# New engine orders, banks and P buffers for a linear-plus-softmax attention mixed with a token MLP; two stores issued by ScalarE

## The chip, the cores and the metric

The kernel runs on one core of one Trainium2 chip. The metric is device time in microseconds of one execution; lower is better. Five engines work side by side and meet through semaphores: TensorE (PE, with its weight loads shown apart as PEld), VectorE (DVE), ScalarE (ACT), GpSimd (POOL) and SyncE (SP), which here only issues DMAs.

## The reference

Two branches read the same 2048 x 448 input `x` and are mixed by a gate for each row. Cut to what matters (16 heads of 28, four segments of 512 rows):

```python
g = sigmoid((x * gate_w).sum(-1, keepdims=True))
# branch A: attention in segments, with a memory of the earlier ones
q, k, v = x @ wq, x @ wk, x @ wv                     # heads, 4 segments of 512
for s in range(4):
    p = softmax(qs @ ks.T * Dh**-0.5 + causal_mask)
    a_dot = p @ vs
    a_mem = (phi(qs) @ M) / (phi(qs) @ z + 1e-6)     # phi(t) = t+1 if t>0 else exp(t)
    o = sigmoid(beta) * a_mem + (1 - sigmoid(beta)) * a_dot
    M, z = M + phi(ks).T @ vs, z + phi(ks).sum()
a = concat(o) @ wo
# branch B: layernorm over 448, then an MLP over the 2048 tokens
u = gelu_tanh(einsum('bsd,sf->bdf', layernorm(x), w1) + b1)   # 448 x 1792
b = (einsum('bdf,fs->bds', u, w2) + b2).T
out = g * a + (1 - g) * b
```

## The kernel before

Everything of one execution is recorded as some 1300 named operations; `ORDER` (from line 288 on) then says, for each engine, in which order it issues them. The order is written out by hand or by a program, not worked out when the kernel is built: `plan` reads the words, `finalize` puts semaphore waits where an operation needs one of another engine. An engine issues strictly in its list's order, so an operation that waits holds up all that stand behind it on its engine. A word like `u3-11*4` means four consecutive operations, `@5` the PSUM bank (or, for `exp`, the P buffer) that the operation takes, `#1` the second operation of that name.

The names that the change and the steps below touch:

- `sc{p}_{f}` on PE (L955): fill `f` (0 to 4) of a pair `p` (0 to 7) of score tiles, four matmuls side by side on 28-row parts of the array, 512 columns, into the four PSUM banks 0 to 3. All 40 fills take these same four banks. `exp{p}_{f}` on ACT (L964) reads all four banks in one instruction of 2048 columns and writes P to one of six P buffers (three more become free in the place of transposed input). `mask{p}_{f}_{j}` on POOL (L967) zeroes the upper triangle of a diagonal block.
- `pv{u}` on PE (L991) multiplies P by V, `mem{u}` reads the memory, `mst{s}` (L830) updates it. `ta{u}`, `tm{u}` (L1007, L1005) transpose the two results on DVE; `eps`, `rec`, `oa`, `om` (L1016 to L1020) and `o{u}` on POOL (L1022) combine them, and `ot{u}` (L1028) transposes the result back. `wo{T}` on PE is the output projection of a 128-row tile `T`; `ag{T}` (L1048 on ACT, L1052 on DVE) takes it out of PSUM with the gate.
- `lo..`, `hi..`, `pr..` on PE: parts of the Q, K and V projections (`lok3_0`, `prq3_1`, `lot10` ...), with `cpk`, `cpq`, `cpv` (L718, L778, L800 and their DVE forms) as evictions. `gt` is the tanh of the gate. `ek`, `eq` (L761, L785) on ACT are the exps of phi for K and Q; `mk`, `phk`, `mq`, `phq` on DVE finish phi.
- `u{ft}-{st}` on PE (L264): the 16 matmuls of 448 columns of each of 14 column tiles of the first MLP product; `ev{ft}` (L1068 on ACT, L1070 on DVE) adds the bias and takes the tile out of PSUM. Three operations on ACT apply Gelu to several tiles at once (L1072): `gl0` to tiles 0 to 4, `gl5` to 5 to 9, `gl10` to 10 to 13. In the trace a load of a function table (`ACT_TABLE_LOAD`) stands ahead of each Gelu and ahead of the next Exp behind it.
- `y{T}-{ft}` on PE: the 14 matmuls of each of 16 output tiles of the second product. `fin{T}` (L1086) on DVE adds the two branches; `out{T}` (L1090) stores the tile by DMA, issued by SP. Tile 15 is made in two parts, columns 0 to 319 and 320 to 447 (`y15-..`, `fin15`, `out15`, and the same names with `#1`).
- `ldw1_{k}_{part}`, `ldw2_{k}_{part}` on SP (L557): quarter loads of the MLP weights into a ring of three slots. `gk..`, `gq..` (L742) gather the last four rows of each head through DRAM, and wait for the copies of K or Q.

A run of whole-array operations that holds a `pv` or `mst` (which use the array in four column tiles) is issued in column tiles too: each matmul then becomes four instructions of 32 columns of weights side by side. `WIDE` (line 286) names two runs which are issued so although they hold none.

Of the kernel before, what the change touches and what calls it, by code (L numbers as in the profile page):

```python
# [5 lines left out]
ACT = mybir.ActivationFunctionType  # L6
# [273 lines left out]
def pool_cost(n):  # L280
# [5 lines left out]
WIDE = ("y1-4", "y0-10",)  # L286
# [3 lines left out]
warm@4 trx0_0@16 warm2 lok0_0@53 trx0_1@72 trx0_1#1 hik0_0 lok0_0h@76 lok0_2@02 hik0_0h hik0_2 lox0_3@41 gtr@6 loq0_1@35 hix0_3  # L290
lot2@67 hiq0_1 hit2 lok1_2@24 loq1_2@01 lok1_0@35 hiq1_2 hik1_0 hik1_2 loq1_0@76 lot0@50 hiq1_0 hit0 lot4@21 lot6@43
hit4 lok2_2@76 btr@0 hit6 prk2_2 prx2_3 u1-0@5 sc0_0@0123 u0-0@4 u1-1 u0-1*2 u1-2*3 u0-3 u1-5 u0-4 u1-6 sc0_1@0123
lok2_0@67 u0-5 prk2_0 prk2_1 u0-6*2 sc0_2@0123 u0-8 u1-7 u0-9 u2-0@6 u1-8 u0-10 u2-1 u1-9*2 u0-11 u2-2 u1-11 u2-3
sc0_3@0123 u2-4 u1-12*2 u0-12 u1-14 u5-0@7 u0-13*2 u5-1 u1-15 u2-5 sc0_4@0123 u0-15 u5-2*2 pv0@5 u2-6*2 u3-0@4 u2-8*2
sc1_0@0123 u2-10 u5-4*2 u4-0@5 u3-1 u2-11 u3-2 u2-12 u4-1 u3-3 u2-13*2 u4-2 sc1_1@0123 u3-4 u5-6*2 u3-5 u5-8 u2-15
u3-6 u4-3 u3-7 u4-4*2 sc1_2@0123 u3-8 u4-6*2 pv1@6 u5-9 u3-9*2 u4-8 u5-10 sc1_3@0123 u3-11 u5-11 u3-12*2 u4-9 u5-12
u3-14*2 u4-10 u6-0@6 u5-13 sc1_4@0123 u7-0@4 u5-14 u6-1 u7-1 u6-2 u4-11 u7-2 u4-12*2 u5-15 u7-3 sc2_0@0123 u6-3 u4-14
u7-4 u4-15 u7-5*2 u6-4*2 u7-7 mst0@7 pv3@0 u6-6 pv2@3 u6-7*3 u7-8 u6-10 loq2_0@57 sc2_1@0123 u7-9 u6-11*3 u7-10 u6-14
prq2_0 u6-15 prq2_1 u7-11*4 sc2_2@0123 loq2_2@75 u8-0@6*2 u7-15 prq2_2 u8-2*5 sc2_3@0123 u8-7*6 prq2_2h u8-13*3
sc2_4@0123 wo1@4 pv4@5 u9-0@6*2 mem4@7 u9-2 sc3_0@0123 u9-3*3 wo0#1@5 u9-6*5 sc3_1@0123 lot8@57 u9-11*5 prt9 prt8  # L300
wo2@0 u10-0@6 u11-0@4 wo3@2 u11-1*2 u10-1 pv5@3 u11-3 u10-2*2 mem5@7 u11-4*3 sc3_2@0123 lot10@57 u10-4 prt11 u10-5
u11-7 prt10 u10-6*2 sc3_3@0123 u12-0@7 u11-8*2 u10-8 u11-10 u10-9 mem6@5 u11-11 u10-10*2 u11-12 sc3_4@0123 u11-13
u12-1 u11-14 u10-12 u12-2 u10-13 u12-3 u13-0@5 u10-14 u11-15 u10-15 sc4_0@0123 u13-1*2 pv6@4 u12-4 u13-3 mem7@6 u12-5
u13-4 u12-6 sc4_1@0123 mst1@4 u13-5*3 u12-7 u13-8*2 u12-8*2 sc4_2@0123 u12-10 pv7@6 u12-11 u13-10*2 u12-12 u13-12
u12-13*2 sc4_3@0123 lok3_0@46 prk3_0 u13-13 u12-15 prk3_1 u13-14 sc4_4@0123 lok3_2@47 u13-15 prk3_2 prx3_3 loq3_0@65
sc5_0@0123 prq3_1 prq3_0 wo7@4 wo5@7 wo4@1 wo6@3 pv8@4 mem8@5 mem9@6 y0-0@7*4 sc5_1@0123 y0-4*2 y2-0@5*3 y0-6 y2-3
y1-0@6*2 y2-4*2 pv9@4 y1-2*2 sc5_2@0123 y1-4 y2-6 y4-0@4*3 y2-7 y0-7*2 y4-3 y0-9 y4-4 y2-8*3 y1-5 sc5_3@0123 y0-10*2
y2-11*2 y1-6*2 y2-13 y1-8*3 y4-5 sc5_4@0123 y0-12*2 y4-6 y1-11*2 y3-0@5 y1-13 y3-1*3 y4-7 sc6_0@0123 y4-8 mem10@6
y5-0@7 y3-4 y4-9 y5-1*2 y4-10 pv10@6 sc6_1@0123 y5-3 y3-5 y5-4 y3-6*3 mem11@6 y3-9 y4-11 y5-5 y4-12 sc6_2@0123 y5-6
y3-10*2 y5-7*4 y4-13 pv11@6 sc6_3@0123 y3-12 y5-11 y7-0@4 y5-12 y7-1 y3-13 y5-13 y6-0@6 y7-2*3 loq3_2@21 lot14@03  # L310
prq3_2 prq3_2h prt14 y7-5*2 prt15 y7-7 y6-1 mst2@5 y7-8 y6-2 sc6_4@0123 lot12@75 y6-3*3 prt13 prt12 y7-9 y6-6*3
sc7_0@0123 y6-9 y7-10 y6-10 y8-0@7 y6-11 y8-1*2 y6-12 y7-11 y6-13 pv12@5 y8-3 y7-12 sc7_1@0123 y7-13 y8-4 wo8@6 pv13@5
mem12@4 y8-5 sc7_2@0123 y8-6 y10-0@6*3 mem13@4 y8-7*3 y10-3 y11-0@5 y8-10 sc7_3@0123 y10-4*2 y11-1 y10-6*2 y11-2 y8-11
wo9@4 y11-3*2 y8-12 sc7_4@0123 y8-13 y11-5 wo11@4 y11-6 pv14@7 y10-8 y12-0@1 y9-0@2 y11-7*2 y13-0@3 y9-1*4 y13-1 y10-9
y9-5 y10-10 mem14@7 y13-2 mem15@0 y11-9 y12-1 wo10@4 y9-6 y13-3 y12-2 y9-7 y10-11 y12-3 y13-4 y9-8 y11-10 pv15@7
y12-4*2 y9-9 y12-6*2 y9-10*2 y12-8 y13-5 y14-0@7 y11-11*2 y14-1 y15-0@0 y9-12 y11-13 y13-6 y9-13 y10-12*2 y14-2*2
y15-1 y13-7 y15-2 y14-4 y12-9 y13-8*2 y15-3 y14-5 y13-10 y12-10 y14-6 y15-4 y14-7 y12-11 y14-8 y13-11*3 y14-9 wo14@5
y14-10 wo12@6 y15-5 y14-11 wo13@5 y12-12 y14-12*2 wo15@6 y15-6*2 y12-13 y15-8*6 y15-0#1@4 y15-1#1 y15-2#1 y15-3#1
y15-4#1 y15-5#1 y15-6#1 y15-7#1 y15-8#1 y15-9#1 y15-10#1 y15-11#1 y15-12#1 y15-13#1
""",  # L320
    "ACT": """
ldx1 ldwkb padx0 xTcp0_01 padx1 xTcp0_11 padq1 cpk0_0 cpk0_2#1 ek0_1 cpk0_0#1 cpq0_2 cpq0_0 gt2 gt3 ln0 cpk1_1 ek0_0
cpk1_3 cpk1_2 cpk1_0 cpq1_2#1 cpq1_3 cpv1 cpq1_1 cpq1_0 gt1 cpv0 gt0 cpv4 gt5 gt4 cpv6 gt6 gt7 cpk2_2 ln7 exp0_0@6
eq1_2 exp0_1@1 cpk2_0 eq1_0 tb exp0_2@5 ln12 exp0_3@7 ek0_2 exp0_4@3 eq1_1 exp1_0@2 eq1_3 mg exp1_1@4 ek0_3 exp1_2@1
exp1_3@6 ek1_0 exp1_4@0 ek1_1 exp2_0@5 gl0 exp2_1@3 ev6 exp2_2@6 ek1_2 exp2_3@4 eq2_0 exp2_4@2 eq2_2 exp3_0@1 ek1_3
exp3_1@5 gl5 gt8 gt9 ek2_0 exp3_2@6 gt11 gt10 exp3_3@3 eq2_1 exp3_4@2 ev11 exp4_0@4 ek2_1 exp4_1@8 exp4_2@7 exp4_3@3
exp4_4@1 cpk3_3 exp5_0@2 gl10 ag4 eq3_0 exp5_1@5 eq2_3 ek2_3 exp5_2@6 exp5_3@3 ek2_2 exp5_4@0 exp6_0@8 eq3_1 exp6_1@2
exp6_2@7 exp6_3@6 eq3_2 cpv15 gt15 gt14 exp6_4@3 gt13 gt12 exp7_0@0 exp7_1@4 eq3_3 exp7_2@3 exp7_3@5 exp7_4@2 ag10
ag15
""",  # L330
    "DVE": """
wo0 padx2 padk2 padk0 xTcp0_00 padk1 bns1 xTcp0_10 bns3 padq0 padq2 cpk0_1 padq3 bns0 bna1 cpk0_1#1 cpk0_2 gw bna0
bns2 bna2 bna3 vpe0 cpk0_3 cpq0_3 cpq0_1 nmr0 cpv2 ln1 ln3 cpv3 ln2 bns5 bns7 cpq1_2 bna5 bns4 bns8 bns10 bns6 bna4
bna8 bns13 bns15 bns11 bna15 bna6 bna7 bns14 vpe4 bns9 bna11 cpv5 b1c b2c nmr4 cpv7 bna9 bna10 vpe8 mk0_0 bns12 cpk2_3
ln4 bna13 ln5 nmr8 ln6 cpq2_3 ln8 phk0_0 bna12 mk0_1 ln9 bna14 ln10 phk0_1 vpe12 cpk2_1 osl ln11 mq1_2 nmr12 ln15 ln13
ln14 maskg0 ev1 ev0 ta0 mk0_2 oc phk0_2 gm mo mq1_1 ev2 rec0 ob0 oa0 mk0_3 gcol0 mq1_3 ta1 phk0_3 ot0 ev3 mk1_0 rec1
phk1_0 oa1 ev5 ot1 omg0 ev4 mq1_0 mstc0 b2g0 gcol1 msta0 ta3 ta2 rec3 phq1_3 phq1_2 phq1_0 rec2 oa2 cpq2_0 cpq2_1 oa3
mk1_1 ev7 cpq2_2 phk1_1 ot2 ot3 cpq2_2#1 mk1_2 ev8 phk1_2 ta4 mq2_0 ag1 tm4 phq1_1 ag0 eps4 rec4 ev9 oa4 cpv9 mq2_2
ag2 cpv8 ag3 omg1 mk1_3 b2g1 ta5 tm5 phq2_0 phk1_3 om4 eps5 cpv11 cpv10 rec5 om5 oa5 tm6 mq2_1 ot4 ev10 ot5 ta6 eps6
mk2_0 rec6 phk2_0 mk2_1 om6 phq2_1 tm7 oa6 eps7 phk2_1 msta1 ta7 rec7 om7 oa7 cpk3_0 ev12 cpk3_1 ev13 cpk3_2 ot7 gcol2  # L340
ot6 cpq3_3 cpq3_1 ag7 cpq3_0 mstc1 ag5 ag6 tm8 ta8 tm9 eps8 rec8 phq2_2 eps9 omg2 ta9 mq3_0 rec9 oa8 om9 mk2_3 phk2_3
mq2_3 oa9 om8 phq2_3 fin2 fin0 fin1 tm10 ot8 eps10 ta10 rec10 mk2_2 tm11 oa10 phk2_2 phq3_0 fin4 mq3_1 ta11 om10 fin3
fin5 ot10 cpq3_2 eps11 cpq3_2#1 cpv14 b2g2 ot9 msta2 phq3_1 rec11 oa11 om11 cpv13 cpv12 mq3_2 phq3_2 mstc2 fin6 ot11
ta12 fin7 ag8 tm12 eps12 ta13 tm13 rec12 eps13 mq3_3 oa12 rec13 ag9 gcol3 om12 fin8 om13 ta14 oa13 phq3_3 ag11 tm14
tm15 eps14 ot13 eps15 ot12 rec14 oa14 ta15 rec15 om15 oa15 om14 omg3 b2g3 ot14 fin9 fin10 fin11 ot15 ag14 ag12 ag13
fin14 fin13 fin12 fin15 fin15#1
""",
    "POOL": """
hm0 id0 v0 hm1 hm2 z3_1 id1 mhalf szb z3_0 szg v1 rstd0 rstd4 hs0 hs27 rstd8 rstd12 mask0_2_2 mask0_1_1 mask0_0_0
mask0_2_2#1 mask0_1_3 mask0_4_1 mask0_4_3 mask0_3_0 mask1_2_2 mask1_0_0 mask1_2_2#1 mask1_3_0 mask1_1_1 mask1_4_1  # L350
mask1_1_3 mask1_4_3 mask2_1_1 mask2_2_2 mask2_0_0 mask2_1_3 mask2_2_2#1 mask3_0_0 mask2_4_1 mask2_4_3 mask3_1_1
mask2_3_0 o4 mask3_1_3 o5 mask3_2_2 mask3_2_2#1 mask3_4_1 mask3_4_3 mask3_3_0 o6 o7 mask4_1_1 mask4_3_0 mask4_4_1
mask4_2_2 mask4_0_0 mask4_1_3 mask4_4_3 mask4_2_2#1 mask5_2_2 mask5_1_1 o8 mask5_0_0 mask5_1_3 mask5_4_1 mask5_2_2#1
mask5_3_0 mask5_4_3 o9 mask6_1_1 mask6_2_2 mask6_1_3 o10 mask6_0_0 o11 mask6_3_0 mask6_2_2#1 mask6_4_1 mask6_4_3
mask7_1_1 mask7_2_2 mask7_1_3 mask7_0_0 mask7_2_2#1 o12 mask7_4_1 mask7_4_3 o13 mask7_3_0 o14 o15
""",
    "SP": """
# [14 lines left out]
def build_kernel(nc, X, WQ, WK, WV, WO, BETA, W1, B1, W2, B2, GW, OUT):  # L372
    NSL, NP = 3, 6
    sch = Sched(nc, {}, {})
    op = sch.op

    x2 = X.rearrange("b s d -> (b s) d")
    out2 = OUT.rearrange("b s d -> (b s) d")
# [45 lines left out]
    outst = sb([128, 4, D])  # L424
# [4 lines left out]
    b1c = sb([128, NFT], F32)  # L429
    b2c = sb([128, NT], F32)  # L430
# [644 lines left out]
    def mm2(T, c0=0, c1=D):  # L1075
# [3 lines left out]
        p = T % 4  # L1079
# [136 lines left out]
```

## Time and profile before

| | us |
|---|---|
| median of 3 runs | 173.01 |
| the runs | 172.37, 173.01, 173.29 |
| the profiled execution's own time | 173.29 |
| its span, first to last instruction | 171.6 |

Of the 40 slices of the span PE is at 80% or more in every one but the last, where it drops to three tenths, and the mean granted TensorE clock is 1.000:

```profile
PE   8899999999999999999999999999999999999993
PEld 3465444444446444453454355544455544566662
DVE  2599999844879998799789999786898996999783
ACT  2434899999899999997997899978846676410010
POOL 8011041455164043432643580079260826542300
DMA  5989795695744944780307547014865265024213
```

Each digit is the busy share of a fortieth of the span, 4.3 us, in tenths. The score fills and their exps lie between the seventh and the thirty-fifth slice, the projections ahead of them, the last MLP tiles behind. The groups of instructions that cost most on ACT and DVE:

```profile
L964 ACT ACTIVATE t<-t 128x2048 bf16<-128x2048 f32 x40 | 75.0, 1876 | 12.3 <-PE t L955 10.3
L1007 DVE STREAM_TRANSPOSE t<-t 128x512 f32<-128x512 f32 x16 | 11.2, 704 | 1.8 <-PE t L991 1.7
L1028 DVE STREAM_TRANSPOSE t<-t 128x512 bf16<-128x512 bf16 x16 | 11.0, 698 | 0.1
```

After the bar stand the busy time in us, the mean of one instruction in ns, then the idle time ahead of the group and what ended it.

### The profile page before, as it was taken

What the parts mean: (1) busy time and instruction counts of PE and PEld (TensorE: products, weight loads), DVE (VectorE), ACT (ScalarE), POOL (GpSimd) and SP (SyncE); (2) the same over time, 40 slices, a digit from 0 to 9 for tenths busy, and PEclk for the clock granted to TensorE, in tenths of its full rate; (3) what the DMA queues carried; (4) which work ended last, traced back from release to release, by engine and by line L of the source; (5) the groups of instructions that cost most, each with busy time, mean ns of one, the idle gap of its engine ahead of it and who ended that gap; (6) DMA issues with size and microseconds to landing.
All of it is one profiled execution on the core that took longest, in us unless ns stands there. A gap on an engine that the chain in (4) does not pass through costs nothing.

```text
span 171.6 us, 5965 instructions
## 1 busy us (share of the span) xinstructions
PE 167.1 (97%) x2571; PEld 85.2 (50%) x2571; DVE 145.1 (85%) x313; ACT 121.7 (71%) x126; POOL 65.6 (38%) x98
## 2 busy tenths in 40 slices
PE   8899999999999999999999999999999999999993
PEld 3465444444446444453454355544455544566662
DVE  2599999844879998799789999786898996999783
ACT  2434899999899999997997899978846676410010
POOL 8011041455164043432643580079260826542300
DMA  5989795695744944780307547014865265024213
GB/s 167 286 158 317 192 285 170 165 262 136 208 120 122 178 94 108 171 237 2 97 0 143 153 140 188 4 31 136 248 181 156 85 188 175 4 61 149 67 57 107
DMA packets 50474, 24.66 MB, mean 144 GB/s; under 512 B 14976, under 2 KB 50208, under 8 KB 50448
## 3 DMA queue, kind: packets, MB, share of 16 engines
q1 hardware_dynamic: 50160, 24.05, 53.9%
q8 instruction: 20, 0.33, 0.8%
q10 hardware_dynamic: 288, 0.23, 0.6%
q14 instruction: 6, 0.05, 0.1%
HBM read 18.76 MB, written 2.36 MB: 123 GB/s over the span
## 4 chain that ended last, share of the span: by engine, by line
PE 91%; DVE 4%; DMA 3%; SPq 0%; ACT 0%; issue 0%
PE t L264 77%; PE t L955 7%; PE t L991 5%; DMA t<-in_A_wk_dram 3%; PE t L830 1%; DVE t L1052 1%; DVE t L802 1%; DVE t L1018 1%; DVE t L1070 0%; DVE t L1007 0%; DVE t L1005 0%; SPq L505 0%; SPq L500 0%; ACT t L667 0%; DVE t L1086 0%
## 5 line engine op out<-in xcount | busy, mean ns | idle before, releaser
L264 PE MATMUL t<-t 128*32 128x448 bf16 (+10 forms) x1839 | 143.3, 346 | 0.7 <-DVE t L617 0.5
L264 PEld LDWEIGHTS t<-t 128*32 128x32 bf16 (+2 forms) x1839 | 69.7, 96 | 60.1 <-issue 10.3
L964 ACT ACTIVATE t<-t 128x2048 bf16<-128x2048 f32 x40 | 75.0, 1876 | 12.3 <-PE t L955 10.3
L967 POOL TENSOR_SCALAR_AFFINE_SELECT t<-t 128x512 bf16<-128x512 bf16 x64 | 42.7, 687 | 44.3 <-ACT t L964 43.9
L1022 POOL TENSOR_TENSOR t<-t 128x448 bf16<-128x448 f32 x12 | 14.8, 1239 | 26.7 <-DVE t L1020 8.2
L955 PE MATMUL t<-t 28*128 28x512 bf16 (+3 forms) x256 | 15.8, 301 | 0.0
L1048 ACT ACTIVATE t<-t 128x448 bf16<-128x448 f32 x3 | 2.2, 718 | 17.9 <-PE t L264 17.9
L1070 DVE TENSOR_SCALAR t<-t 128x448 bf16<-128x448 f32 x12 | 8.2, 681 | 6.9 <-PE t L264 6.6
L904 POOL TENSOR_TENSOR t<-t 128x4 f32<-128x4 f32 x4 | 4.1, 1015 | 22.7 <-DVE t L902 22.7
L1007 DVE STREAM_TRANSPOSE t<-t 128x512 f32<-128x512 f32 x16 | 11.2, 704 | 1.8 <-PE t L991 1.7
L1052 DVE TENSOR_SCALAR t<-t 128x448 bf16<-128x448 f32 x13 | 9.5, 737 | 3.1 <-PE t L264 3.0
L1086 DVE SCALAR_TENSOR_TENSOR t<-t 128x448 bf16<-128x448 f32 (+2 forms) x17 | 10.6, 645 | 1.1 <-PE t L264 1.0
L955 PEld LDWEIGHTS t<-t 28*128 28x128 bf16 x256 | 4.5, 92 | 14.2 <-ACT t L964 10.3
L991 PE MATMUL t<-t 128*32 128x512 bf16 (+3 forms) x256 | 11.5, 299 | 0.0
L1028 DVE STREAM_TRANSPOSE t<-t 128x512 bf16<-128x512 bf16 x16 | 11.0, 698 | 0.1
L1018 DVE SCALAR_TENSOR_TENSOR t<-t 128x448 f32<-128x448 f32 x12 | 9.9, 826 | 0.1
L1005 DVE STREAM_TRANSPOSE t<-t 128x512 f32<-128x512 f32 x12 | 8.3, 699 | 1.5 <-PE t L264 1.5
L991 PEld LDWEIGHTS t<-t 128*32 128x32 bf16 x256 | 6.8, 97 | 4.9 <-issue 0.4
L895 DVE BATCH_NORM_STATS2 t<-t 128x6 f32<-128x448 bf16 x16 | 9.2, 604 | 0.0
L785 ACT ACTIVATE t<-t 128x512 bf16<-128x512 bf16 x12 | 7.5, 624 | 2.3 <-DVE t L776 2.3
L765 DVE SCALAR_TENSOR_TENSOR t<-t 128x512 bf16<-128x512 bf16 x12 | 8.7, 724 | 0.0
L1020 DVE TENSOR_TENSOR t<-t 128x448 f32<-128x448 f32 x12 | 8.1, 678 | 0.1
(72 smaller groups left out, 127.3 us busy)
## 6 DMA issues: line engine op xcount, KB each, us to landing
t<-in_B_w_dram SPq DMA_DIRECT2D x52, 256.0 KB, 3.5
out_dram<-t SPq DMA_DIRECT2D x15, 112.0 KB, 2.5
t<-in_A_x_dram SPq DMA_DIRECT2D x3, 448.0 KB, 4.3
t<-in_B_w_dram SPq DMA_DIRECT2D x8, 128.0 KB, 2.5
t<-in_A_wo_dram SPq DMA_DIRECT2D x4, 98.0 KB
t<-in_A_wq_dram SPq DMA_DIRECT2D x1, 336.0 KB, 4.9
t<-in_A_wv_dram SPq DMA_DIRECT2D x1, 336.0 KB, 5.2
spare_heads<-t SPq DMA_DIRECT2D x8, 32.0 KB
```

The source lines that it names most:

```text
L264: last = e.matmul(out[q], w[:, q], x, skip_group_check=True, **kw)
L895: op("DVE", lambda e: e.bn_stats(st6[:, t, :], xh[:, t, :]), reads=[R_x[t]], writes=[R_st6[t]], name=f"bns{t}", cost=512, prio=P_PROJ - 10 ...
L955: last = e.matmul(bank(fb[hl])[:, c0 : c0 + w], kT[r, hg, s * 512 + j * 128 : s * 512 + j * 128 + 128], qT[r, hg, s * 512 + 128 * j : s * ...
L964: op("ACT", lambda e: e.activation(pslot(g), ps[:, fb[0].bank : fb[0].bank + 4, :], ACT.Exp, scale=SCALE), use=fb, reads=[bres(b) for b in ...
L967: op("POOL", lambda e, c0=c0: e.affine_select(pslot(g)[:, :, c0 : c0 + 128], pslot(g)[:, :, c0 : c0 + 128], pattern=[[0, 4], [1, 128]], co ...
L991: last = e.matmul(bank(cb)[32 * hl : 32 * hl + 32, 128 * j : 512], vaug[:, 4 * s + j, 32 * h : 32 * h + 32], pslot(P_fill[u // 2][f])[:, h ...
L1007: dv(lambda e: e.transpose(t2[:, 0, :], bank(cb)[:, 0:512]), [bres(cb)], [R_tt[tb][0]], "ta", 630, use=(cb,))
L1018: dv(lambda e: e.scalar_tensor_tensor(n3[0], n3[0], oc, rb[0], op0=ALU.mult, op1=ALU.mult), [R_tt[tb][0], R_rec[tb], R_omcol], [R_tt[tb][0 ...
L1022: op("POOL", lambda e: e.tensor_tensor(o3, n3[0], n3[1], op=ALU.add), reads=R_tt[tb], writes=[R_ob[tb]], name=f"o{u}", cost=1280, port=Tru ...
L1028: dv(lambda e: e.transpose(oT[:, hg, s * 512 : s * 512 + 512], o), [R_ob[tb]], qres(hg, s), "ot", 635)
L1052: alt=("DVE", lambda e: e.tensor_scalar(ag(T), bank(b)[:, 0:D], gcol[:, T : T + 1], b2g[:, T : T + 1], op0=ALU.mult, op1=ALU.add), dve_cos ...
L1086: op("DVE", lambda e: e.scalar_tensor_tensor(outst[:, p, c0:c1], bank(b)[:, 0 : c1 - c0], omg[:, T : T + 1], ag(T)[:, c0:c1], op0=ALU.mult ...
```

## The change

All five lists of `ORDER` are written anew: the same operations in another order, with other PSUM banks and P buffers. Some evictions and small operations change between ACT and DVE: `ag10`, `ag4`, `ev11`, `mg`, `ln12`, `cpv15`, `cpq0_0`, `cpq1_1`, `cpk2_0`, `cpk3_3` and three small ones leave ACT's list for DVE's, and 27 others come over from DVE's (`ag1`, `ag2`, `ag11`, `ag13`, `ag14`, `ev5`, `ev8`, `ev9`, `ln11`, `ln13` and evictions of K, Q and V among them). `WIDE` is empty. The stores of tile 12 and of the first part of tile 15 are issued by ACT, at the end of its list, instead of by SP. The diff, cut to the lines that matter below:

```diff
-WIDE = ("y1-4", "y0-10",)
+WIDE = ()
 ORDER = {
     "PE": """
...
-hit4 lok2_2@76 btr@0 hit6 prk2_2 prx2_3 u1-0@5 sc0_0@0123 u0-0@4 u1-1 u0-1*2 u1-2*3 u0-3 u1-5 u0-4 u1-6 sc0_1@0123
...
-u3-14*2 u4-10 u6-0@6 u5-13 sc1_4@0123 u7-0@4 u5-14 u6-1 u7-1 u6-2 u4-11 u7-2 u4-12*2 u5-15 u7-3 sc2_0@0123 u6-3 u4-14
-u7-4 u4-15 u7-5*2 u6-4*2 u7-7 mst0@7 pv3@0 u6-6 pv2@3 u6-7*3 u7-8 u6-10 loq2_0@57 sc2_1@0123 u7-9 u6-11*3 u7-10 u6-14
-prq2_0 u6-15 prq2_1 u7-11*4 sc2_2@0123 loq2_2@75 u8-0@6*2 u7-15 prq2_2 u8-2*5 sc2_3@0123 u8-7*6 prq2_2h u8-13*3
...
-wo2@0 u10-0@6 u11-0@4 wo3@2 u11-1*2 u10-1 pv5@3 u11-3 u10-2*2 mem5@7 u11-4*3 sc3_2@0123 lot10@57 u10-4 prt11 u10-5
-u11-7 prt10 u10-6*2 sc3_3@0123 u12-0@7 u11-8*2 u10-8 u11-10 u10-9 mem6@5 u11-11 u10-10*2 u11-12 sc3_4@0123 u11-13
-u12-1 u11-14 u10-12 u12-2 u10-13 u12-3 u13-0@5 u10-14 u11-15 u10-15 sc4_0@0123 u13-1*2 pv6@4 u12-4 u13-3 mem7@6 u12-5
-u13-4 u12-6 sc4_1@0123 mst1@4 u13-5*3 u12-7 u13-8*2 u12-8*2 sc4_2@0123 u12-10 pv7@6 u12-11 u13-10*2 u12-12 u13-12
...
-u12-13*2 sc4_3@0123 lok3_0@46 prk3_0 u13-13 u12-15 prk3_1 u13-14 sc4_4@0123 lok3_2@47 u13-15 prk3_2 prx3_3 loq3_0@65
-sc5_0@0123 prq3_1 prq3_0 wo7@4 wo5@7 wo4@1 wo6@3 pv8@4 mem8@5 mem9@6 y0-0@7*4 sc5_1@0123 y0-4*2 y2-0@5*3 y0-6 y2-3
-y1-0@6*2 y2-4*2 pv9@4 y1-2*2 sc5_2@0123 y1-4 y2-6 y4-0@4*3 y2-7 y0-7*2 y4-3 y0-9 y4-4 y2-8*3 y1-5 sc5_3@0123 y0-10*2
...
-y15-1 y13-7 y15-2 y14-4 y12-9 y13-8*2 y15-3 y14-5 y13-10 y12-10 y14-6 y15-4 y14-7 y12-11 y14-8 y13-11*3 y14-9 wo14@5
-y14-10 wo12@6 y15-5 y14-11 wo13@5 y12-12 y14-12*2 wo15@6 y15-6*2 y12-13 y15-8*6 y15-0#1@4 y15-1#1 y15-2#1 y15-3#1
-y15-4#1 y15-5#1 y15-6#1 y15-7#1 y15-8#1 y15-9#1 y15-10#1 y15-11#1 y15-12#1 y15-13#1
...
+lot4@72 btr@3 hiq1_0 hit6 hit4 lok2_2@46 prk2_2 prx2_3 sc0_0@0123 u0-0@5*5 u1-0@4*7 u0-5 sc0_1@0123 lok2_0@67 u1-7
...
+u3-0@7 u4-6*2 u3-1*3 pv1@4 u4-8*3 sc1_2@0123 u3-4*2 u4-11*2 u6-0@4*4 u4-13*3 u3-6 u6-4 sc1_3@0123 u5-9*3 u3-7*4 u7-0@5
+u6-5 u5-12 u3-11*4 sc1_4@0123 u3-15 u7-1*4 u5-13*3 u7-5*3 sc2_0@0123 mst0@7 u7-8*8 pv2@6 u6-6*6 pv3@6 sc2_1@0123
+loq2_0@57 u6-12*4 prq2_1 prq2_0 sc2_2@0123 loq2_2@46 prq2_2 u9-0@5*2 prq2_2h u9-2*2 u8-0@7*2 mem4@4 sc2_3@0123 u8-2*7
...
+u9-13*3 prt9 pv5@6 wo3@5 sc3_2@0123 lot10@46 mem5@7 prt11 u11-0@5*2 prt10 u10-0@7 u11-2 u10-1 sc3_3@0123 u10-2 mem6@4
+u10-3*2 u11-3*3 u10-5 u11-6*3 sc3_4@0123 u10-6*2 pv6@4 u11-9*3 u12-0@6*2 u11-12 u10-8 u13-0@4 u12-2*2 u13-1*3
+sc4_0@0123 u11-13 u10-9*2 u13-4*2 u11-14*2 u10-11 u12-4 u10-12*3 sc4_1@0123 mst1@5 u12-5*3 u13-6 u12-8 u10-15 mem7@5
...
+u12-9 sc4_2@0123 u12-10*6 u13-7*2 pv7@5 sc4_3@0123 lok3_0@67 prk3_1 prk3_0 u13-9*4 sc4_4@0123 lok3_2@57 prk3_2 prx3_3
+u13-13*3 sc5_0@0123 loq3_0@65 prq3_0 prq3_1 wo5@7 mem8@4 sc5_1@0123 pv8@5 wo6@6 y0-0@4 wo7@7 y0-1 y1-0@5 y0-2*2
+sc5_2@0123 mem9@6 y1-1*3 wo4@7 y0-4*4 y1-4*2 pv9@6 sc5_3@0123 y0-8 y2-0@7*4 y3-0@6*3 y0-9 y3-3*2 y2-4 y0-10 y3-5
...
+y14-0@2 y11-5 y14-1 y9-10 y14-2*2 y9-11*2 y13-0@0 y9-13 y13-1*2 y14-4 y10-10 mem15@1 y14-5*2 pv15@3 y13-3 y11-6 y14-7
+y13-4*2 y11-7*4 wo10@1 y14-8 y13-6*2 y10-11*2 y13-8*2 wo11@7 y11-11 y15-0@1*2 y14-9*2 y13-10 y11-12 y13-11 y10-13
+y11-13 y13-12*2 y12-13 wo14@7 y15-2*2 y14-11 y15-4*3 wo12@4 y15-7 wo13@6 wo15@3 y15-8*2 y14-12*2 y15-10*4 y15-0#1@4
+y15-1#1 y15-2#1 y15-3#1 y15-4#1 y15-5#1 y15-6#1 y15-7#1 y15-8#1 y15-9#1 y15-10#1 y15-11#1 y15-12#1 y15-13#1
 """,
     "ACT": """
...
-eq1_2 exp0_1@1 cpk2_0 eq1_0 tb exp0_2@5 ln12 exp0_3@7 ek0_2 exp0_4@3 eq1_1 exp1_0@2 eq1_3 mg exp1_1@4 ek0_3 exp1_2@1
-exp1_3@6 ek1_0 exp1_4@0 ek1_1 exp2_0@5 gl0 exp2_1@3 ev6 exp2_2@6 ek1_2 exp2_3@4 eq2_0 exp2_4@2 eq2_2 exp3_0@1 ek1_3
-exp3_1@5 gl5 gt8 gt9 ek2_0 exp3_2@6 gt11 gt10 exp3_3@3 eq2_1 exp3_4@2 ev11 exp4_0@4 ek2_1 exp4_1@8 exp4_2@7 exp4_3@3
-exp4_4@1 cpk3_3 exp5_0@2 gl10 ag4 eq3_0 exp5_1@5 eq2_3 ek2_3 exp5_2@6 exp5_3@3 ek2_2 exp5_4@0 exp6_0@8 eq3_1 exp6_1@2
-exp6_2@7 exp6_3@6 eq3_2 cpv15 gt15 gt14 exp6_4@3 gt13 gt12 exp7_0@0 exp7_1@4 eq3_3 exp7_2@3 exp7_3@5 exp7_4@2 ag10
-ag15
...
+exp0_0@0 ln7 exp0_1@1 ln11 cpk2_1 exp0_2@2 ln13 exp0_3@3 exp0_4@4 eq1_1 exp1_0@5 eq1_0 ek0_2 exp1_1@0 ek0_3 exp1_2@1
+eq1_3 exp1_3@2 ek1_0 exp1_4@3 ev5 gl0 ek1_1 exp2_0@4 exp2_1@0 ev6 cpq2_0 exp2_2@1 ek1_2 exp2_3@2 eq2_0 eq2_1 exp2_4@0
+ag1 exp3_0@3 ev8 exp3_1@4 gt8 ev9 gt9 ag2 exp3_2@0 ek2_0 ek1_3 gt10 exp3_3@1 eq2_2 gt11 exp3_4@2 gl5 exp4_0@3 exp4_1@4
+exp4_2@5 exp4_3@0 cpk3_1 cpk3_0 exp4_4@1 cpk3_2 exp5_0@2 cpq3_1 gl10 exp5_1@3 eq3_0 ek2_1 eq3_1 eq2_3 exp5_2@4
+exp5_3@0 exp5_4@1 ek2_3 ek2_2 exp6_0@5 exp6_1@2 exp6_2@3 exp6_3@6 cpq3_2 cpq3_2#1 eq3_2 gt15 gt14 exp6_4@0 cpv12 gt12
+cpv13 gt13 exp7_0@1 exp7_1@2 exp7_2@0 eq3_3 exp7_3@3 exp7_4@4 ag11 ag13 ag14 ag15 out12 out15
 """,
     "DVE": """
...
-ta12 fin7 ag8 tm12 eps12 ta13 tm13 rec12 eps13 mq3_3 oa12 rec13 ag9 gcol3 om12 fin8 om13 ta14 oa13 phq3_3 ag11 tm14
-tm15 eps14 ot13 eps15 ot12 rec14 oa14 ta15 rec15 om15 oa15 om14 omg3 b2g3 ot14 fin9 fin10 fin11 ot15 ag14 ag12 ag13
-fin14 fin13 fin12 fin15 fin15#1
...
+mstc2 rec11 gcol3 ta12 oa11 om11 ot10 fin7 ot11 fin6 ta13 phq3_2 ag9 phq3_0 ag8 fin8 tm13 omg3 b2g3 eps13 rec13 oa13
+om13 tm12 eps12 mq3_3 rec12 phq3_3 oa12 om12 tm14 ta14 eps14 rec14 ot13 oa14 tm15 eps15 ta15 om14 rec15 ot12 fin9 ag10
+om15 oa15 ot14 ot15 fin11 fin10 ag12 fin12 fin13 fin14 fin15 fin15#1
 """,
...
     "SP": """
...
-dtx2_0 dtx2_1 ldw1_0_0 ldw1_0_2 ldw1_0_1 ldw1_0_3 ldw1_1_0 gk0_1 ldw1_2_0 ldwo2 gq0_3 gk0_0 gk0_3 gq0_0 ldw1_1_1 gq0_2
...
-ldw2_7_1 ldw2_7_2 out8 ldw2_7_3 out10 out9 out11 out14 out13 out12 out15 out15#1
...
+dtx2_0 dtx2_1 ldw1_0_0 ldw1_2_0 ldw1_0_2 ldwo2 gk0_2 ldw1_0_1 ldw1_1_3 gq0_1 ldw1_2_2 ldw1_1_0 ldw1_0_3 gk0_3 gk0_0
...
+gq3_h0 out4 gq3_h2 gq3_h1 ldw2_6_1 ldw2_4_3 ldw2_6_3 ldw2_6_0 out7 ldw2_6_2 out8 ldw2_5_3 out6 ldw2_7_0 ldw2_7_1
+ldw2_7_2 ldw2_7_3 out5 out11 out9 out10 out13 out14 out15#1
 """,
 }
...
            name=f"fin{T}", cost=dve_cost(c1 - c0) + 60, prio=P_BASE)
-        op("SP", lambda e: e.dma_start(out2[T * 128 : T * 128 + 128, c0:c1], outst[:, p, c0:c1]),
+        op("ACT" if (T, c0) in ((12, 0), (15, 0)) else "SP", lambda e: e.dma_start(out2[T * 128 : T * 128 + 128, c0:c1], outst[:, p, c0:c1]),
            reads=[R_outst[4 if c0 else p]], name=f"out{T}", dma=True, out=True, cost=500, nbytes=256 * (c1 - c0))
 
     def mm2_last(T):
```

The lists of POOL follow those of the other engines in the same way (`mask`, `o` and a few small operations in another order), and the left-out lines of PE, ACT, DVE and SP hold the rest of the same operations.

## What the change will do to the time

> **What bounds the kernel now.** I read the head of the page first, then the chain of work that ended last.
>
> ```profile
> span 171.6 us, 5965 instructions
> ...
> PE 167.1 (97%) x2571; PEld 85.2 (50%) x2571; DVE 145.1 (85%) x313; ACT 121.7 (71%) x126; POOL 65.6 (38%) x98
> ```
>
> TensorE is busy for 97% of the span and sets the end. A busy PE need not be a PE at its peak, so I price its work from stretches of the chain in order of time (start, length, what):
>
> ```profile
> 33.73 0.33 PE t L955 x4
> 34.06 2.19 PE t L264 x11
> 36.25 0.33 PE t L955 x8
> 36.58 0.68 PE t L264 x12
> 37.26 0.54 PE t L991 x16
> 37.80 0.95 PE t L264 x20
> 38.75 0.33 PE t L955 x4
> 39.07 2.57 PE t L264 x13
> ```
>
> L955 is a score fill (`sc`), L264 the MLP matmuls, L991 a `pv`. Eleven MLP matmuls take 2.19, thirteen 2.57: 0.19 each, and 0.10 for the change of array tiling ahead of the next fill. A fill is 0.33 with its own change, a `pv` 0.54; 512 columns are 0.19 x 512/448 = 0.22, a `wo` is 4 x 0.19 = 0.76. With these prices the stretches fit with no room: PE has work, changes of tiling, and almost no waits. So reordering can win little in the middle, and every new PE wait goes to the end in full.
>
> The second thing to see is who stands next to PE. All fills use banks 0 to 3, so a fill cannot start before the exp of the fill ahead of it has read them. The waits show that handshake (weights of a fill, held by an exp):
>
> ```profile
> PEld t L955 <- ACT t L964: 10.3, 29, 0.4
> ```
>
> Then I asked for the stretches that hold the Gelu activations, here `gl0` and `gl10` (columns: window, length, busy PE, PEld, DVE, ACT, POOL):
>
> ```profile
> 51.30:58.40 7.10, 7.10 (x180) 3.91 (x178) 6.66 (x16) 6.93 (x6) 1.82 (x3) 1.00 0.97 153
> 98.90:106.30 7.40, 7.40 (x156) 3.83 (x156) 7.28 (x13) 7.27 (x7) 3.32 (x6) 1.00 0.65 174
> ```
>
> There ScalarE is as full as TensorE (6.93 of 7.10, 7.27 of 7.40), although over the span it is at 71%. Its timeline in the first one says why:
>
> ```profile
> 51.33 0.62 ACT L761 ACTIVATE t<-t 128x512 bf16<-128x512 bf16 x1
> 52.07 1.88 ACT L964 ACTIVATE t<-t 128x2048 bf16<-128x2048 f32 x1
> 53.96 1.28 ACT L1072 ACT_TABLE_LOAD   x1
> 55.26 2.07 ACT L1072 ACTIVATE t<-t 128x2240 bf16<-128x2240 bf16 x1
> 57.34 1.28 ACT L964 ACT_TABLE_LOAD   x1
> 58.64 1.88 ACT L964 ACTIVATE t<-t 128x2048 bf16<-128x2048 f32 x1
> 60.41 0.63 ACT L1068 ACTIVATE t<-t 128x448 bf16<-128x448 f32 x1
> ```
>
> and the fill ahead of that exp in the chain:
>
> ```profile
> 51.69 0.33 PE t L955 x4
> ```
>
> A Gelu between two exps costs its own 2.07 and two function table loads of 1.28, laid end to end with 0.01 to 0.02 between. Ordinary activations overlap the one ahead by 0.11 (60.41 against 58.64 + 1.88). An exp starts 0.38 after its fill (52.07 against 51.69). Before, `sc2_0`, `sc3_1` and `sc5_0` are followed by enough PE work that ACT is free again when the next exp is due.
>
> **The change part by part.**
>
> *PE's own work.* The same 618 items; counted from the lists, 95 changes of tiling before and 95 after (with `WIDE` empty two runs go back to whole-array matmuls, priced alike above). Cost 0.
>
> *Gelu places.* In the new ACT list they stand between `exp1_4` and `exp2_0`, `exp3_4` and `exp4_0`, `exp5_0` and `exp5_1`, and PE's list has no wide interval between fills at these places. I lay ACT's rows end to end from the start of the fill ahead of the Gelu to the end of the exp behind it, and PE's rows over the same two intervals.
>
> `mst0` comes from the chain too:
>
> ```profile
> 53.83 0.50 PE t L830 x64
> ```
>
> `gl0`: exp1_4 0.38 to 2.26, ev5 to 2.78, load to 4.08, gl0 to 6.17, load to 7.46, ek1_1 to 8.10, exp2_0 to 9.88. PE reaches `sc2_1` after 0.33 + 11 x 0.19 + 0.10 = 2.52 and 0.33 + 0.50 + 14 x 0.19 + 2 x 0.54 + 0.10 = 4.67, so at 7.19. Late by 2.7.
>
> `gl5`: exp3_4 to 2.26, load 3.56, gl5 5.65, load 6.94, exp4_0 8.84. PE reaches `sc4_1` after 0.33 + 15 x 0.19 + 0.54 + 0.10 = 3.82 and 0.33 + 12 x 0.19 + 0.10 = 2.71, so at 6.53. Late by 2.3.
>
> `gl10`: exp5_0 to 2.26, then `cpq3_1` and `gl10`, priced by these rows of groups:
>
> ```profile
> L1072 ACT ACTIVATE t<-t 128x1792 bf16<-128x1792 bf16 x1 | 1.7, 1698 | 0.0
> ```
>
> ```profile
> L778 ACT ACTIVATE t<-t 128x512 bf16<-128x512 f32 x4 | 2.2, 596 | 2.4 <-PE t L264 2.4
> ```
>
> the copy to 2.75, load 4.05, gl10 5.77, load 7.06, exp5_1 8.96. PE reaches `sc5_2` after 0.33 + 0.10 + `loq3_0` 0.22 + 0.10 + six passes 1.30 + `wo5` 0.76 + `mem8` 0.22 = 3.03 and 0.33 + 0.54 + 2 x 0.76 + 5 x 0.19 + 0.10 = 3.44, so at 6.47. Late by 2.5. Four 0.62 activations then stand between exp5_1 and exp5_2, which makes exp5_2 end 3.86 behind exp5_1 while `sc5_3` is due at 3.71 (0.33 + `mem9` 0.22 + 9 x 0.19 + 0.76 + 0.54 + 0.10, from 0.05): 0.2 more.
>
> The hand-over from exp to fill is not shown in a tight place; between 0 and 0.12, I take 0.05. A waiting PE has drained already, which saves the 0.10. So 2.65 + 2.25 + 2.45 + 0.2 = **7.55**. Behind each waiting fill stands the whole rest of PE's list, and it cannot be caught up since no later stretch of PE has slack. No other term of the change comes near this.
>
> The Trainium skill bears on this price (ScalarE: Activation LUTs, What ACT_TABLE_LOAD costs): a switch to another set of functions costs about 1283 ns for the load and some 1380 ns for a drain. The trace agrees on the load; a drain does not appear in it, since the next activation starts 0.02 behind the load. What the drain would make of the sum stands at rival 4.
>
> *ACT and DVE shares.* Net 14 evictions and the like move from DVE (313 instructions) to ACT, about 14 x 0.6 = 8 us each way. ACT goes to some 130 of 171 us; outside the three places above its work per fill interval stays under the interval or is caught up in the next. DVE only gets looser. Cost 0.
>
> *A wait that goes.* `lot10` waited for a transpose of DVE:
>
> ```profile
> 78.07 0.40 PE L955 MATMUL t<-t 28*128 28x256 bf16 x8
> 78.58 0.85 PE L264 MATMUL t<-t 64*128 64x449 bf16 x4
> ```
>
> ```profile
> 77.93 0.61 DVE t L1005
> ```
>
> The fill at 78.07 needs 0.33, the transpose ended at 78.54, and `lot10` began at 78.58: PE lost 0.18. In the new list other work stands there: gain 0.2.
>
> *Weights.* The second quarter of the first W1 slot (`ldw1_0_1`) now stands behind `gk0_2`, which waits for the last K copies, on SP. SP's timeline:
>
> ```profile
> 18.49 2.78 SPq L557 DMA_DIRECT2D t<-in_B_w_dram  x5
> 21.31 0.65 SPq L742 DMA_DIRECT2D spare_heads<-t  x1
> ```
>
> and L557's answer for 18.4 to 22.6 gives the time from issue to landing:
>
> ```profile
> DMA to landing us min/median/max: 3.2/4.7/5.4
> ```
>
> Issued at about 21.6 to 22 instead of 19.7 it lands at 26.3 to 27.4. `u0-4` comes behind the first fill, which the chain has at
>
> ```profile
> 25.70 0.33 PE t L955 x4
> ```
>
> and which now stands ahead of the one MLP matmul that preceded it: 25.5 + 0.33 + 4 x 0.19 = 26.6. Cost 0 to 0.8, I take 0.3. The rest of the first 25 us keeps its order nearly: between -0.3 and +0.3, I take 0.
>
> *The end.* The chain's last step, and SP's timeline:
>
> ```profile
> 168.71 0.35 DVE t L1086
> ```
>
> ```profile
> 169.01 0.45 SPq L1090 DMA_DIRECT2D out_dram<-t  x1
> 169.51 0.45 SPq L1090 DMA_DIRECT2D out_dram<-t  x1
> ```
>
> The last piece is done at 169.06 but its store goes out at 169.51, behind the first part's on SP. With that part and tile 12 on ACT, SP is free at 169.1: gain 0.4. ACT issues its two behind `ag15`, where nothing else waits; its stores, issued no later than SP's last, land no later than about when that one does. Between `pv15` and `wo14` PE has 27 x 0.19 + 2 x 0.76 + 0.27 = 6.9; the string on DVE and POOL up to `ot15` took 7.3 from the end of `pv15` before, by these rows of the chain and of DVE's timeline:
>
> ```profile
> 154.28 0.54 PE t L991 x16
> ```
>
> ```profile
> 161.40 0.70 DVE L1028 STREAM_TRANSPOSE t<-t 128x512 bf16<-128x512 bf16 x1
> ```
>
> It loses two `fin` and the gate columns and gains `ot12` and `ag10`: late by 0 to 0.6, I take 0.1.
>
> Sum: 7.55 - 0.2 + 0.3 - 0.4 + 0.1 = +7.35. The profiled execution took 173.29 with its span of 171.6, so 180.6; it stands 0.28 over 173.01, the median of the runs shown, so **180.4**.
>
> **The rivals.**
>
> 1. *Not slower: ACT does not pay the loads.* If the new order left Exp and Gelu in one resident table, 2.6 would fall off each block; the first fill would be late by 0.05 and the others not. Then 173.01 - 0.2 + 0.05 = 172.9. It decides only when both loads of a block go: with one left, 1.3 + 1.0 + 1.2 stay, about 176. For it: ACT as a whole has room (71%). Against it: the loads are there at every change of function in the trace, and the new list has an Exp on both sides of each Gelu.
>
> 2. *More waits than these.* The new lists were laid tightly; a bank, a P buffer or a gather that comes late elsewhere adds to PE, most likely where ACT's new evictions hold banks. 1 to 3 on top: 181.4 to 183.4. Against it: each of the three stalls gives every other engine 2 us of slack.
>
> 3. *The clock falls in the stalls.* The first matmuls ran slowly:
>
> ```profile
> 0.83 3.15 PE L606 MATMUL t<-const-bfloat16-1.0 128*128 128x512 bf16 x7 [0.83 <-PEq L1201]
> ```
>
> 0.45 each against 0.22. If an idle of 2.5 brought that back, each stall would lose at least what these seven lost, 7 x 0.23 = 1.6, and thrice that is 4.8: 185. No wait of such length is in the middle of this trace, so no row excludes it. By the Trainium skill (TensorE: Matmul & The Clock Gate, What's actually happening) the clock drops after an idle window of about 3.4 us, which speaks against it; no row here shows that.
>
> 4. *A pause behind each load.* The rows leave 0.02 between a load and the next activation, six times, so 0.1 in all: 180.5. By the drain that the page on ScalarE named above states, an estimate of 6 x 1.38 us, it would be about 188; the rows nearly exclude it.
>
> **How the numbers follow.** Forecast 0.78 at 180.4; rival 1 0.07; rival 2 0.10; rival 3 0.04; rival 4 0.01. The forecast's own bounds (hand-over, weights, tail, the first 25 us, 0.5 between runs) make 178.4 to 182; with rival 2 the range is 178.4 to 183.4. Half a per cent (0.87) is about what a measurement of this kernel can tell from no change. Faster by more needs rival 1 with luck: 0.02; within 0.05; slower 0.93.
>
> **What would show it.** Right: PE waits of 2.2 to 2.7 ahead of `sc2_1`, `sc4_1`, `sc5_2`, put down to L964, two table loads and a Gelu of ACT on the chain each time; seven loads in all; PE busy about as before in a span near 178.9; the last store issued within 0.1 of its piece. Wrong: fewer loads, waits of PE elsewhere, or MLP matmuls slower than 0.19 behind a stall.

## The result, and the profile after

The changed kernel took 185.62 us, the median of four runs (185.63, 185.60, 185.81, 183.56), against 173.08 before: a ratio of 1.0705, 95% interval 1.0623 to 1.0787. The forecast was 180.4 with a range up to 183.4. The sign and the main cause were right; the time is 5.2 us above the forecast and outside its range, because a second cause, a fall of the clock, was not in the sum. The profiled execution took 185.63 with a span of 183.5, so 12.34 us more than the profiled one of before (173.29), 11.9 of it in the span.

The head of the page of the changed kernel, with its row of the granted clock and its chain:

```profile
span 183.5 us, 5638 instructions
...
PE 170.0 (93%) x2400; PEld 86.0 (47%) x2406; DVE 137.9 (75%) x299; ACT 128.8 (70%) x140; POOL 65.0 (35%) x98
...
PEclk9999999999999699999987999999999999999999
...
PE 72%; ACT 16%; SPq 4%; DMA 3%; issue 2%; DVE 1%; ACTq 0%
```

Before, the chain was PE almost throughout:

```profile
PE 91%; DVE 4%; DMA 3%; SPq 0%; ACT 0%; issue 0%
```

Now 16% of it is ScalarE, and the row of the clock has two notches, in slice 14 and in slices 21 and 22 of 40 (4.59 us each). PE's busy time grew by 2.9 although it does the same items: the notches are in it.

The waits name who held PE (total, times, longest):

```profile
PE t L949 <- ACT t L958: 6.3, 3, 2.7
...
PE t L264 <- ACT t L1066: 1.1, 1, 1.1
PE t L949 <- DMA t<-spare_heads: 1.0, 1, 1.0
```

Three fills (L949) wait for an exp (L958); one MLP matmul waits for a Gelu itself (L1066); one fill waits for a DMA. The MLP matmul is `y0-0`: the first matmul of every output tile is recorded as reading all 14 column tiles, so the first one needs the last Gelu, `gl10`. ScalarE's timeline at the first place shows what the exp stood behind (start, length, what):

```profile
50.71 1.88 ACT L958 ACTIVATE t<-t 128x2048 bf16<-128x2048 f32 x1 [0.69 <-PE t L949]
52.49 0.63 ACT L1062 ACTIVATE t<-t 128x448 bf16<-128x448 f32 x1
53.13 1.28 ACT L1066 ACT_TABLE_LOAD   x1
54.43 2.07 ACT L1066 ACTIVATE t<-t 128x2240 bf16<-128x2240 bf16 x1
56.52 1.28 ACT L755 ACT_TABLE_LOAD   x1
57.81 0.63 ACT L755 ACTIVATE t<-t 128x512 bf16<-128x512 bf16 x1
58.35 1.86 ACT L958 ACTIVATE t<-t 128x2048 bf16<-128x2048 f32 x1
```

This is the forecast's row for `gl0` piece by piece: from the fill, 0.38 ahead of the first row, to the end of the last exp at 60.21 it is 9.88. PE's timelines at the three Gelu places:

```profile
60.26 0.40 PE L949 MATMUL t<-t 28*128 28x384 bf16 x8 [2.68 <-ACT t L958]
60.59 2.03 PE L264 MATMUL t<-t 64*128 64x512 bf16 x6
...
94.13 0.40 PE L949 MATMUL t<-t 28*128 28x384 bf16 x8 [2.36 <-ACT t L958]
...
112.06 1.89 PE L264 MATMUL t<-t 128*32 128x448 bf16 x36 [1.09 <-ACT t L1066]
115.21 0.40 PE L949 MATMUL t<-t 28*128 28x256 bf16 x8 [1.26 <-ACT t L958]
```

Set against the normal step from one matmul to the next, the losses are a little more than the idle times in brackets, which go by modelled ends: 2.77 ahead of `sc2_1`, 2.42 ahead of `sc4_1`, 1.26 ahead of `y0-0` and 1.35 ahead of `sc5_2`, and 0.19 ahead of `sc5_3`: 7.99 in all. What the forecast did not have is the second of those lines: six matmuls that take 2.03. The windows of the changed kernel show why (the column behind the five engines is the granted clock):

```profile
60.80:61.00 0.20, 0.20 (x3) 0.05 (x2) 0.00 (x0) 0.20 (x1) 0.11 (x1) 0.53 0.32 105
61.00:64.00 3.00, 2.78 (x9) 1.11 (x9) 0.06 (x1) 2.22 (x2) 1.28 (x2) 0.50 0.38 98
64.20:64.40 0.20, 0.20 (x3) 0.07 (x1) 0.20 (x1) 0.00 (x0) 0.00 (x0) 0.93 0.00 0
94.80:95.00 0.20, 0.20 (x41) 0.20 (x34) 0.00 (x0) 0.20 (x1) 0.20 (x1) 0.87 1.12 300
95.00:98.00 3.00, 3.00 (x46) 1.12 (x34) 2.47 (x4) 1.45 (x1) 2.89 (x4) 0.50 0.33 85
```

A 0.2 us window whose mean is 0.53 fell to 0.50 after 0.01, so the clock fell at 60.81; by the same reading it rose at 64.23 and fell again at 94.95. The first dip lasted 3.41 us, and by the windows the second too (0.60 in 98.20:98.40, so it ended at 98.36); in each PE lost half of that, 1.7.

The fifth wait, 1.07 ahead of `sc7_2`, is on the chain with the DMAs that hand over the q of the last segment:

```profile
144.49 3.85 DMA spare_heads<-t
...
149.54 1.66 DMA t<-spare_heads
151.21 0.24 issue
151.45 0.40 PE t L949 x8
```

The sum along PE: 7.99 + 3.4 + 1.07, less 0.19 (the wait of `lot10` is gone) and 0.6 (the chain has the first fill at 24.91; before, at 25.70 with one MLP matmul of 0.19 ahead of it), is 11.7; PE's last matmuls end 11.7 later (180.38 in the chain against 168.69). Behind PE stand 0.2 more in the span and 0.4 outside it (time less span is 2.13, before 1.69).

### The profile page after: what moved, and what is told of

The parts are those of the page before. It is cut to its first block, busy times and chain, and to the rows that moved or that the text cites. A ratio compares the mean times of both kernels' runs of the same rounds, so it can differ in the third digit from the quotient of the medians.

```text
span 183.5 us, 5638 instructions
## 1 busy us (share of the span) xinstructions
PE 170.0 (93%) x2400; PEld 86.0 (47%) x2406; DVE 137.9 (75%) x299; ACT 128.8 (70%) x140; POOL 65.0 (35%) x98
## 3 DMA queue, kind: packets, MB, share of 16 engines
HBM read 18.76 MB, written 2.36 MB: 115 GB/s over the span
## 4 chain that ended last, share of the span: by engine, by line
PE 72%; ACT 16%; SPq 4%; DMA 3%; issue 2%; DVE 1%; ACTq 0%
PE t L264 60%; PE t L949 6%; ACT t L958 6%; ACT t L1066 3%; PE t L600 2%; PE t L985 2%; ACT L1066 2%; DMA spare_heads<-t 2%; ACT L958 1%; SPq L551 1%; SPq L741 1%; DMA t<-spare_heads 1%; ACT t L779 1%; SPq L736 1%; PE t L644 1%
## 5 line engine op out<-in xcount | busy, mean ns | idle before, releaser
L264 PE MATMUL t<-t 128*32 128x448 bf16 (+8 forms) x1668 | 145.0, 350 | 2.1 <-ACT t L1066 1.1
L264 PEld LDWEIGHTS t<-t 128*32 128x32 bf16 (+2 forms) x1674 | 70.5, 98 | 62.6 <-issue 14.4
L958 ACT ACTIVATE t<-t 128x2048 bf16<-128x2048 f32 x40 | 75.1, 1877 | 19.4 <-PE t L949 18.9
L1016 POOL TENSOR_TENSOR t<-t 128x448 bf16<-128x448 f32 x12 | 14.1, 1172 | 35.4 <-DVE t L1014 29.8
L949 PE MATMUL t<-t 28*128 28x512 bf16 (+3 forms) x256 | 15.9, 303 | 7.4 <-ACT t L958 6.3
L1042 ACT ACTIVATE t<-t 128x448 bf16<-128x448 f32 x6 | 4.1, 723 | 15.8 <-PE t L264 15.8
L949 PEld LDWEIGHTS t<-t 28*128 28x128 bf16 x256 | 4.5, 92 | 22.0 <-ACT t L958 13.7
L1046 DVE TENSOR_SCALAR t<-t 128x448 bf16<-128x448 f32 x10 | 7.4, 736 | 4.7 <-PE t L264 4.7
L1064 DVE TENSOR_SCALAR t<-t 128x448 bf16<-128x448 f32 x10 | 6.6, 664 | 4.5 <-PE t L264 4.4
L784 DVE SCALAR_TENSOR_TENSOR t<-t 128x512 bf16<-128x512 bf16 x12 | 8.8, 742 | 0.0
L759 DVE SCALAR_TENSOR_TENSOR t<-t 128x512 bf16<-128x512 bf16 x12 | 8.2, 681 | 0.1
L1012 DVE SCALAR_TENSOR_TENSOR t<-t 128x448 f32<-128x448 f32 x12 | 8.0, 668 | 0.1
L1014 DVE TENSOR_TENSOR t<-t 128x448 f32<-128x448 f32 x12 | 7.6, 630 | 0.0
```

The costliest lines, as they stand in the source:

```text
L264: last = e.matmul(out[q], w[:, q], x, skip_group_check=True, **kw)
L784: op("DVE", lambda e: e.scalar_tensor_tensor(ph, qs, 0.0, ph, op0=ALU.max, op1=ALU.add), reads=qres(hg, tc) + [R_phq[hg][tc]], writes=[R_p ...
L949: last = e.matmul(bank(fb[hl])[:, c0 : c0 + w], kT[r, hg, s * 512 + j * 128 : s * 512 + j * 128 + 128], qT[r, hg, s * 512 + 128 * j : s * ...
L958: op("ACT", lambda e: e.activation(pslot(g), ps[:, fb[0].bank : fb[0].bank + 4, :], ACT.Exp, scale=SCALE), use=fb, reads=[bres(b) for b in ...
L1016: op("POOL", lambda e: e.tensor_tensor(o3, n3[0], n3[1], op=ALU.add), reads=R_tt[tb], writes=[R_ob[tb]], name=f"o{u}", cost=1280, port=Tru ...
```

## The experiments

My theory after the result: the two table loads of each Gelu make the exp behind it late because the fill intervals there are narrow (8.0); the waits of over 2 us bring the clock down (3.4); the gathers of the last q are late (1.07). The rivals were ScalarE's extra evictions and the new P buffers for the first, and any other cause of the dips for the second.

**No table loads, new orders** (`a1_tanh_after`)

```diff
-            op("ACT", lambda e: e.activation(uT[:, lo:hi, :], uT[:, lo:hi, :], ACT.Gelu_apprx_tanh), reads=R_uT[lo:hi],
+            op("ACT", lambda e: e.activation(uT[:, lo:hi, :], uT[:, lo:hi, :], ACT.Tanh), reads=R_uT[lo:hi],
```

> The changed kernel with Tanh in place of Gelu in its three places, so that no function table has to be loaded between exp and the activation; the output leaves Gelu out. Theory (the stalls of PE ahead of sc2_1, sc4_1 and sc5_2 are the two loads of each block, and the dips of the clock follow from those stalls): the waits of 2.8, 2.4 and 2.6 us go to 0.2 or less, no dip of the clock, 174.6 us (185.6 less 8.0 less 3.4, with the wait of 1.07 ahead of sc7_2 left in place). Rival A (the stalls come from ScalarE's extra evictions or from the new P buffers): waits of over 1.5 stay, 180 to 185. Rival B (the clock dips for other reasons than the stalls): stalls go, dips stay, 177.6 to 178.

The kernel applies Tanh where the reference has Gelu; its trace has one table load, at the start, in place of seven. 174.94 us, ratio 1.0117 (1.0079 to 1.0156), clock 1.0. PE's timeline at the first place has no wait left:

```profile
57.31 0.73 PE L985 MATMUL t<-t 128*32 128x512 bf16 x16
57.97 0.40 PE L949 MATMUL t<-t 28*128 28x384 bf16 x8
58.30 2.55 PE L264 MATMUL t<-t 64*128 64x512 bf16 x12
```

The fill follows the `pv` at once and the matmuls behind it run at full speed. With the same evictions on ScalarE and the same P buffers the 8.0 and the 3.4 are gone, so rivals A and B fall. What is left over before is 2.1 by the medians and 1.6 between the two profiled executions (174.90 against 173.29). The 1.6 lies in three places: PE ends 0.6 later (small waits, the largest 0.42 ahead of `lok3_0`), the time from there to the end of the span is 0.6 longer (the last store, below), and 0.4 lies outside the span. The wait ahead of `sc7_2`, which the expectation left in place, is not in this profile, so that its 174.6 is nearly met is in part luck.

**No table loads, old orders** (`a2_tanh_before`; the same edit in the kernel before)

> The kernel before with the same Tanh in place of Gelu; the output leaves Gelu out. Theory (before, each Gelu block lay beside a fill interval wide enough, so that PE waited for no load): 173.0, within 0.3. Rival (the loads cost before too, hidden in small waits spread over the lists): each of the six loads gives back up to 1.28, 166 to 171.

172.89 us, ratio 1.0002 (0.9983 to 1.0020). Here too Tanh stands where the reference has Gelu. Before, the six loads cost nothing, all 7.7 us of them lay beside PE's work. The price is not that of the load; it is that of the place.

**The place alone** (`b1_gl5_narrow`; kernel before, ScalarE's list)

```diff
-exp3_1@5 gl5 gt8 gt9 ek2_0 exp3_2@6 gt11 gt10 exp3_3@3 eq2_1 exp3_4@2 ev11
+exp3_1@5 gt8 gt9 ek2_0 exp3_2@6 gt11 gt10 exp3_3@3 gl5 exp3_4@2 eq2_1 ev11
```

> The kernel before with one word moved: in ScalarE's list gl5 stands between exp3_3 and exp3_4, where the fill interval is 2.5 us, instead of behind exp3_1, where it is 7.25; eq2_1 goes behind exp3_4. Theory (a Gelu with its two loads costs nothing in a wide interval and the whole lateness in a narrow one): from the start of sc3_3, exp3_3 ends at 2.26, load 3.55, gl5 5.63, load 6.92, exp3_4 8.81, and sc4_0 is due at 5.02, so TensorE waits 3.8 ahead of sc4_0, the clock falls to half for 3.4 us behind that wait (1.7), and the extra 0.5 of eq2_1 may cost 0.3: 178.3 to 178.7 us, clock about .99. Rival (the stalls of the changed kernel come from its other lists, and one Gelu in a narrow interval is caught up): 172.8 to 174.

178.53 us, ratio 1.0342 (1.0315 to 1.0369), clock .98 to .99. ScalarE's timeline, PE's timeline and a window:

```profile
84.52 2.07 ACT L1072 ACTIVATE t<-t 128x2240 bf16<-128x2240 bf16 x1
86.60 1.28 ACT L964 ACT_TABLE_LOAD   x1
```

```profile
89.83 0.52 PE L955 MATMUL t<-t 28*128 28x512 bf16 x4 [3.82 <-ACT t L964]
```

```profile
90.20:93.00 2.80, 2.80 (x40) 1.26 (x40) 2.67 (x6) 2.80 (x4) 1.51 (x3) 0.50 0.00 0
```

One Gelu moved by two exps (and `eq2_1` by one, behind `exp3_4`), with every other list as it was, gives the wait that the ledger says (3.8) and a stretch at half clock behind it. It costs 5.7 us by the medians.

**Work in place of the wait** (`a3_dummy_pe`; changed kernel)

```diff
-... pv2@6 u6-6*6 pv3@6 sc2_1@0123
+... pv2@6 u6-6*6 pv3@6 dumA@7 sc2_1@0123
-... u12-4 u10-12*3 sc4_1@0123 mst1@5
+... u12-4 u10-12*3 dumB@5 sc4_1@0123 mst1@5
+    def dummy(name, n):
+        b = Bank()
+        def fn(e):
+            for _ in range(n):
+                last = e.matmul(bank(b), ones[:, 0:128], ones, start=True, stop=True, skip_group_check=True)
+            return last
+        op("PE", fn, writes=[bres(b)], take=b, use=(b,), name=name, mode="f", cost=n * pe_cost(512))
+    dummy("dumA", 10)
+    dummy("dumB", 9)
```

> The changed kernel with ten matmuls of 512 columns ahead of sc2_1 and nine ahead of sc4_1, into a bank that nothing reads then: they fill the two waits with PE work and add none of use. Theory (PE's idle brings the clock down to half for 3.4 us, which costs 1.7 each time): the fills start where they did, within 0.2, the clock stays at 1.0 and the time is 182.2. Rival (the clock falls for another reason, such as the load of the chip at that time, or the dummy work counts as no work): dips at about 61 and 95 us stay, 185.6.

182.61 us, ratio 1.0559 (1.0535 to 1.0584), clock 1.0 but for .998 in the profiled run. PE's timeline and a window behind the fill:

```profile
58.12 2.36 PE L611 MATMUL t<-const-bfloat16-1.0 128*128 128x512 bf16 x10
60.90 0.40 PE L961 MATMUL t<-t 28*128 28x384 bf16 x8 [0.42 <-ACT t L970]
```

```profile
61.00:64.00 3.00, 3.00 (x28) 1.13 (x24) 0.83 (x2) 2.58 (x3) 1.18 (x3) 1.00 0.43 121
```

The fill is no earlier in its stretch: `sc2_0` to `sc2_1` takes 7.48, as in the changed kernel. But the clock stays up: from `sc2_1` to `sc2_2` it takes 2.81 where the changed kernel took 4.45, and from `sc4_1` to `sc4_3` 4.98 where it took 6.58. The kernel is 3.0 us faster, for 19 matmuls that compute nothing. So the dips at these places come from PE's idle.

**Less work in place of the wait** (`b4_dummy_less`; the same kernel with 3 and 5 dummies)

```diff
-    dummy("dumA", 10)
-    dummy("dumB", 9)
+    dummy("dumA", 3)
+    dummy("dumB", 5)
```

> The changed kernel with three dummy matmuls ahead of sc2_1 and five ahead of sc4_1 in place of ten and nine, so that TensorE still waits about 2.1 and 1.3 us. Theory (the clock is judged by the share of idle in a stretch of 3.4 us, and 1.3 of it was seen to leave the clock alone): no dip behind sc4_1, and the dip behind sc2_1 tells whether 2.1 is enough; 183.9 with one dip, 182.2 with none. Rival (any wait of over 1 us at these places brings the clock down): two dips, 185.6.

183.73 us, ratio 1.0638 (1.0611 to 1.0664), clock 1.0 in both runs:

```profile
60.26 0.40 PE L961 MATMUL t<-t 28*128 28x384 bf16 x8 [1.97 <-ACT t L970]
...
92.48 0.40 PE L961 MATMUL t<-t 28*128 28x384 bf16 x8 [1.26 <-ACT t L970]
```

Neither wait brought the clock down, so the rival, by which any wait of over 1 us here would do so, falls. The expected 182.2 was not reached though: later waits, 0.6 ahead of `sc7_2` (gather) and 0.8 ahead of `y12-0` (weights), are in this profile and not in that of `a3_dummy_pe`.

**The gathers moved forward** (`b2_gather_early`; changed kernel, SP's list)

```diff
-tk2_3 ldw2_4_2 tk2_2 ldw2_4_1 gq3_3 gk3_h0 gk3_h1 ldw2_3_2 ldw2_5_1 ldw2_4_0 gq3_0 out3 gq3_2 ldw2_5_0 ldw2_5_2 gq3_1
+tk2_3 ldw2_4_2 tk2_2 ldw2_4_1 gq3_3 gk3_h0 gk3_h1 gq3_0 gq3_2 gq3_1 ldw2_3_2 ldw2_5_1 ldw2_4_0 out3 ldw2_5_0 ldw2_5_2
```

> The changed kernel with the three gathers gq3_0, gq3_2 and gq3_1 directly behind gk3_h1 in SP's list, ahead of five weight loads and a store. Theory (the wait of 1.07 ahead of sc7_2 is these gathers' place on SP: the second stage could not be issued before 148.4): the wait goes and nothing follows it, 184.55 us. Rival (the gathers wait for SP's issue of gk3_h0 and for the transfers in flight, not for their place): the wait stays within 0.3, 185.6.

185.39 us, ratio 1.0756 (1.0715 to 1.0798); no gain that can be told. PE's timeline:

```profile
143.61 1.12 PE L264 MATMUL t<-t 128*128 128x448 bf16 x5 [1.33 <-DMA t<-in_B_w_dram]
...
150.61 0.40 PE L949 MATMUL t<-t 28*128 28x256 bf16 x8
```

The wait ahead of `sc7_2` went, as the theory has it, but the weight loads that were pushed back are now late ahead of `sc7_0`: 1.33, where the wait that went was 1.00. Both theories missed this. Two of the four runs had one dip fewer (mean clock .991 and .989), as one of the changed kernel's had; between runs with the same number of dips this order was 0 to 1.6 us slower (185.64 and 186.53 against 185.60 to 185.81; 185.07 and 185.15 against 183.56).

The place on SP is not the whole cause of the wait either. `a1_tanh_after`, `a3_dummy_pe` and `b3_tail_order` have the changed kernel's place for these gathers, and no wait ahead of `sc7_2` in their profiles. There SP issued the next DMA 2.7 to 3.1 us after `gq3_1`, in the changed kernel 3.9 us after it. So the 1.07 is a wait of this profile, and comes and goes from run to run; why the transfer took longer is not shown.

This run, `b2_gather_early`, also shows something of the clock. Its waits at the Gelu places are those of the changed kernel, but its profile has one dip only (windows behind the first wait and across the second):

```profile
60.88 0.40 PE L949 MATMUL t<-t 28*128 28x384 bf16 x8 [2.72 <-ACT t L958]
...
93.10 0.40 PE L949 MATMUL t<-t 28*128 28x384 bf16 x8 [2.36 <-ACT t L958]
```

```profile
61.00:64.00 3.00, 3.00 (x28) 1.11 (x20) 0.85 (x2) 2.61 (x3) 1.19 (x3) 1.00 0.32 93
94.20:94.40 0.20, 0.20 (x12) 0.13 (x8) 0.20 (x1) 0.20 (x1) 0.20 (x2) 0.70 0.94 274
95.00:97.00 2.00, 2.00 (x28) 0.74 (x20) 2.00 (x3) 0.42 (x1) 1.90 (x3) 0.50 0.12 28
```

The longer wait left the clock alone, the shorter one did not. The last section comes back to it.

**The two stores alone** (`a4_stores_before`; kernel before)

```diff
-ag15
+ag15 out12 out15
-... out9 out11 out14 out13 out12 out15 out15#1
+... out9 out11 out14 out13 out15#1
-        op("SP", lambda e: e.dma_start(...
+        op("ACT" if (T, c0) in ((12, 0), (15, 0)) else "SP", lambda e: e.dma_start(...
```

> The kernel before with one part of the change alone: the stores of tile 12 and of the first part of tile 15 issued by ScalarE at the end of its list, all orders as they were. Theory of the prediction's step: out15#1 no longer stands behind out15 on SP, issued within 0.1 of its piece, 0.4 gained, 172.6. Rival (SP's issue ahead of it, out13 or out14, takes 1.2 to 1.4 us whenever it is the second one after a pause, and is still running when the last piece is done): nothing gained, 173.0, within 0.2.

172.53 us in 12 runs, ratio 0.9981 (0.9962 to 0.9999). The last piece, 0.35 on DVE from 168.72, is done at 169.07. SP's timeline:

```profile
169.10 0.33 SPq L1090 DMA_DIRECT2D out_dram<-t  x1
```

Its store goes out at 169.10, where before it went out at 169.51. The gain is 0.3; the interval just leaves out no change. It is the only edit here that was faster than the kernel before.

In the changed kernel's profile the same edit gains nothing; no run took it out there. Its chain and SP's timeline:

```profile
180.41 0.35 DVE t L1080
```

```profile
179.81 1.87 SPq L1084 DMA_DIRECT2D out_dram<-t  x2
```

The last piece is done at 180.76; the two issues are `out14`, which holds SP for 1.39, and `out15#1`, which starts at 181.25. `out14` is the second store behind a pause of SP, and such a one took 0.33 to 1.94 in the profiles of these kernels. In `a1_tanh_after` it held SP until 170.52, 0.87 behind the last piece.

**Another sharing out of the last stores** (`b3_tail_order`; on `a3_dummy_pe`)

```diff
-... ag13 ag14 ag15 out12 out15
+... ag13 ag14 ag15 out13 out15
-... out9 out10 out13 out14 out15#1
+... out9 out10 out12 out14 out15#1
-... in ((12, 0), (15, 0)) else "SP"
+... in ((13, 0), (15, 0)) else "SP"
```

> The kernel with the ten and nine dummy matmuls, and the stores shared out in another way: tile 13 and the first part of tile 15 on ScalarE, tiles 12 and 14 and the last part of tile 15 on SP. Theory (on a queue that has paused, the second store holds its engine for 0.4 to 1.9 us, and in the changed kernel this is out14, 0.3 to 0.9 ahead of the last piece): SP's second store is issued earlier, out15#1 goes out within 0.1 of its piece in every run, and the time is 182.1 to 182.2 against 182.6. Rival (the long issue belongs to whatever stands ahead of the last store, or ScalarE's out15 is held in its place): 182.6 or more.

Four runs: 182.16, 183.83, 181.86, 181.90, median 182.03 against 182.61. Three lie at or below the 182.1 to 182.2 of the theory and one does not; the profiles of both kernels show `out15#1` issued 0.03 behind its piece, so they do not tell. Inconclusive.

## Why the prediction was wrong, step by step

- *Three Gelu places, 7.55.* Right in mechanism, places and size: 7.99, shown by `a1`, `a2` and `b1`. One detail was off: at `gl10` PE stopped twice, first `y0-0` for the Gelu itself (1.26) and then `sc5_2` (1.35); the ledger had only the fill, and nearly the same sum (2.61 against 2.45). That the sum still fits is luck: the need of `y0-0` for the last Gelu was overlooked.
- *The step that failed: rival 3 was left out of the sum.* It was priced at 1.6 for each stall and given 0.04; the runs show 1.7 for two of the three, 3.4 of the 5.2 that are missing (`a3_dummy_pe` fills two waits and both dips go). Its sign of being wrong, slower matmuls behind a stall, came true: 4.45 from `sc2_1` to `sc2_2` against 2.81 with the waits filled. The text had said that no row excluded it, and then let a rule decide: the Trainium skill (TensorE: Matmul & The Clock Gate, What's actually happening) puts the drop behind an idle window of about 3.4 us, which I read as an idle of that length. The trace disagrees with that reading: a wait of 2.36 was enough. The Trainium skill calls that window, in the same section, free-running and 3413 ns long; the trace agrees, with dips of 3.41 each.
- *Rival 2, waits elsewhere, 0.10.* It came true as well in this profile: 1.07 ahead of `sc7_2`, at its lower price of 1 to 3; three profiles with the same place for the gathers have no such wait. The case against it, that each stall gives the other engines slack, does not reach these gathers: they start from a copy (`cpq3_2`, at 136.89) right behind the PE work that it takes out, and queue on SP.
- *The tail, -0.4.* The step is right for the edit alone (-0.3 in `a4`), wrong for this order: the forecast took every store on SP at 0.45 and did not ask how long the one ahead of the last would hold the engine. *The tail string, +0.1:* no such loss in this profile.
- *`lot10`, -0.2:* right. *Weights, +0.3:* no wait at `u0-4` in this profile. *Prologue, 0 ± 0.3:* -0.6, of which 0.4 from weights of k that landed earlier (the copy on DVE that waits for them began at 5.77 against 6.18); with the same lists the first fill started anywhere from 24.5 to 25.6 in the profiles of these kernels, so it is chance.
- *Evictions moved to ScalarE, 0:* nearly right; `a1` has some 0.9 of small waits in all, most of them hidden behind the stalls of the changed kernel.
- *Rivals 1 and 4:* seven loads are there, and the activation behind a load of a Gelu place starts 0.01 to 0.02 later, as forecast. Rival 4's estimate has a slip: 6 x 1.38 on top of 180.4 is 188.7, not 188.
- *What stays open.* The time outside the span is 2.0 to 2.2 in the runs with the new orders and 1.7 to 1.9 in those with the old ones (with the stores on ScalarE too), 0.4 that no view here explains. And one of 23 runs of the kernel before took 174.09 at a mean clock of .990, which is what one dip gives, though the profiled execution of that kernel has no wait of PE of over 0.2 us behind its first 10 us; no trace of that run is kept.

## What to carry to other kernels

A function table load was free here where the consumer's interval was wide enough; where it was not, six of them, 7.7 us in all, cost 8.0 of waiting and 3.4 of clock: lay the engine's rows end to end from one handshake to the next and compare with the work of the other side, at each place. A wait of PE of over 2 us has to be priced with the clock that it may lose, here 1.7 on top of 2.4; filling it with work that computes nothing won 3.0 of 185.6. And reordering a queue that is late need not mend it: in the one run of this kind here the transfers that were pushed back were the next ones late.

## What the hardware showed that I had not expected

The clock falls and rises on a grid of its own. In the changed kernel it rose at 64.23 and fell at 94.95, 30.72 apart, nine times 3.41, and each dip lasts one step of it. The fall behind that kernel's last matmul lies on it too: at 183.69 (0.73 in 183.60:183.80), 26 steps from 94.95.

What decides, by these traces, is how much of a wait falls into one step. In the changed kernel the waits of 2.68 and 2.36 lie whole inside the steps that ended at 60.81 and 94.95, and the clock fell. In `b2_gather_early` the fall is at 94.28 (0.70 in a 0.2 us window), and 2.2 of the wait of 2.36 lies in the step that ended there. Ten steps back from it lies 60.15, and this cuts the wait of 2.72 that ended at 60.88 into 2.0 and 0.7: no dip. In `b4_dummy_less` the wait of 1.97 says less than it seems to: the clock fell at 181.61, behind the last matmul (0.53 in 181.60:181.80), and 36 steps and 35 steps back lie 58.73 and 62.15, so this wait, which ended at 60.26, was cut into 0.4 and 1.5.

So 2.2 us of idle in one step cost the clock and 2.0 did not, and a longer wait may cost it or not by where the grid cuts it: the changed kernel's run at 183.56 had a mean clock of .991 where the three others had .981, one dip fewer. This reading is worked out from those few times; no run set the length of a wait inside one step by itself.
